# Attention and gated MLP on one core: heads in pairs, 64-row score tiles, and one written order for TensorE

## The chip, the cores and the metric

The kernel runs on one core of a Trainium2 chip. The metric is the device time of one execution in microseconds (us), median of several runs.

## What is computed

Sliding-window attention with ALiBi (a bias that falls linearly with the distance of query and key, with a slope for each head), and behind it a two-layer MLP with a swish gate. Batch 8, 8 heads, 576 tokens, 64 columns a head; 4608 tokens of 512 columns enter the MLP, whose inner width is 2048. All inputs and the output are fp32.

```python
scores = scale * np.matmul(q, k.transpose(0, 1, 3, 2))
slopes = 2.0 ** (-8.0 * (np.arange(H, dtype=np.float32) + 1) / H)
bias = slopes[:, None, None] * (-np.abs(rel).astype(np.float32))[None, :, :]
mask = (rel >= 0) & (rel < window)          # window = 128
scores = np.where(mask, scores + bias[None], -1000000000.0)
attn = np.exp(scores - max); attn = attn / sum(attn)
x = np.matmul(attn, v)                      # to (4608, 512)
h = x @ w_in
g = h * (1.0 / (1.0 + np.exp(-beta * h)))
out = g @ w_out
```

## The kernel before, in words

The work goes batch by batch. `emit_loads` (L72 to L95) brings q, k and v of a batch into bf16 tiles `qs`, `ks`, `vs`, with a cast during the transfer, all issued by GpSimd (POOL); so are both weight matrices (L144, L145). Batch b+1 is loaded while batch b is worked on. The loads, then the weights, stand in POOL's queue ahead of the small identity `identf` (L148) by which TensorE transposes beta (L152).

ALiBi is put into the score product: four more columns (L238, L239, from the tables `QA` and `KBH`) follow the 64 of each head, so that q and k have 68 rows after their transposition. TensorE transposes one head of 128 tokens at a time (L245, L253) into PSUM, and VectorE (DVE) copies eight heads at once to `qT` and `kT` (L248, L256).

For a block `kb` of 128 keys (the fifth has 64) and a pair of heads, two matmuls (L270) give the scores against the key block's own queries and those of the next block, at most 256 columns, in the PSUM tile `sps`, of which there are two. ScalarE (ACT) makes one exponential of both heads (L281, L294), DVE multiplies by a 0/1 mask (L287, L300), and the result `pt` holds probabilities by key. For each block of queries, matmuls with `pt` as the stationary operand (L318, L327) give 64 columns of output and, from a column of ones in `vs`, the sum; DVE divides (L335, L336); four transposes (L345) and a DVE copy (L350) put the 512 columns of these tokens into the ring `XT`.

When 512 tokens are complete, `emit_moe_group` (L176) runs the MLP for them. Stage one: for each of 16 blocks of inner columns, four matmuls of 512 columns to `hps` (L184; two PSUM buffers), a tanh on ACT with a scale per partition (L192), and on DVE (tanh + 1) * h to `gT` (L198). Stage two: for each of four blocks of 128 tokens, 16 matmuls to `ops` (L211; one PSUM buffer), scaling by 0.5 on DVE (L219), and a store on SyncE's queue (SP, L221).

The order on each engine comes from the framework's scheduler, which mixes the instructions of these stages as it lists them. A transpose, score product or pv product of a short block has 64 rows or columns in its operands; all other TensorE work has up to 128 of both and uses the whole array.

Of the kernel before, what the change touches and what calls it, by code (L numbers as in the profile page):

```python
# [14 lines left out]
P = 128  # L15
# [3 lines left out]
def kernel(  # L19
# [16 lines left out]

    NQB = 5
    SPAD = NQB * P
    AUG = 4
    DA = D + AUG  # L40
    DPITCH = 80
# [3 lines left out]
    NTG = (T + TOKG - 1) // TOKG  # L45
    XTR = min(NTG, 3) * TOKG
    slopes = [2.0 ** (-8.0 * (h + 1) / H) for h in range(H)]
    qscale = 1.0 / sqrt(D)

# [4 lines left out]
    beta_sb = const.tile([P, NFF], F32, name="beta_sb")  # L54
    mask = const.tile([P, 2, 2, P], BF16, name="mask")
    QA = const.tile([P, NQB, AUG], BF16, name="QA")
    KB = const.tile([P, NQB, AUG], BF16, name="KB")
    KBH = const.tile([P, NQB, H, AUG], BF16, name="KBH")
    const.seal()

    xt_pool = ctx.enter_context(tc.tile_pool(name="xtbuf", bufs=1))
    XT = xt_pool.tile([P, NDM, XTR], BF16, name="XT")
    xt_pool.seal()
    wt_pool = ctx.enter_context(tc.tile_pool(name="wts", bufs=1))
    W1 = wt_pool.tile([P, NDM, DFF], BF16, name="W1")
    W2 = wt_pool.tile([P, NFF, DM], BF16, name="W2")
    wt_pool.seal()

    make_identity(nc, ident[:])

    stage = ctx.enter_context(tc.tile_pool(name="stage", bufs=2))
    qt_pool = ctx.enter_context(tc.tile_pool(name="qtkt", bufs=2))  # L72

    stage_tiles = {}

    def emit_loads(b):
        qs = stage.tile([P, NQB, H, DPITCH], BF16, name="qs", tag="qs")
        ks = stage.tile([P, NQB, H, DPITCH], BF16, name="ks", tag="ks")
        vs = stage.tile([P, NQB, H, DPITCH], BF16, name="vs", tag="vs")
        for sb in range(NQB):  # L80
            rows = P if sb < 4 else 64
            for src, dst in ((q, qs), (k, ks)):
                nc.gpsimd.dma_start(  # L83
                    out=dst[0:rows, sb, :, 0:D],
                    in_=src[b, :, 128 * sb : 128 * sb + rows, :].rearrange("h p d -> p h d"),
                )
        for h in range(H):
            nc.gpsimd.dma_start(  # L88
                out=vs[:, 0:4, h, 0:D],
                in_=v[b, h, 0:512, :].rearrange("(kb p) d -> p kb d", p=P),  # L90
            )
        nc.gpsimd.dma_start(
            out=vs[0:64, 4, :, 0:D],
            in_=v[b, :, 512:576, :].rearrange("h p d -> p h d"),
        )  # L95
        stage_tiles[b] = (qs, ks, vs)

    nc.vector.memset(mask[:], 1.0)
    nc.gpsimd.affine_select(
        out=mask[:, :, 0, :],  # L100
        in_=mask[:, :, 0, :],
        compare_op=ALU.is_ge,
        fill=0.0,
        base=0,
        pattern=[[0, 2], [1, P]],
        channel_multiplier=-1,
    )
    nc.gpsimd.affine_select(
        out=mask[:, :, 1, :],
        in_=mask[:, :, 1, :],  # L110
        compare_op=ALU.is_ge,
        fill=0.0,
        base=-1,
        pattern=[[0, 2], [-1, P]],
        channel_multiplier=1,
    )

    nc.vector.memset(QA[:, :, 0:2], 1.0)
    nc.vector.memset(KB[:, :, 2:4], 8.0)
    for sb in range(NQB):  # L120
        lo_off = 128 * (sb % 2)
        hi = 256 * (sb // 2)
        nc.gpsimd.iota(
            QA[:, sb, 2:3],
            pattern=[[0, 1]],
            base=-lo_off,
            channel_multiplier=-1,
            allow_small_or_imprecise_dtypes=True,
# [100 lines left out]
    for b in range(B):  # L229
        qs, ks, vs = stage_tiles[b]  # L230
        if b + 1 < B:
            emit_loads(b + 1)
# [155 lines left out]
```

## Time and profile before

| what | value |
|---|---|
| runs of the kernel, us | 450.35, 449.67, 446.89; median 449.67 |
| span of the profiled execution, us | 447.5 (no other time of it is on record) |
| PE, DVE, ACT, POOL busy | 92%, 61%, 39%, 28% of the span |
| mean granted clock of TensorE | 0.934 of full speed |
| bytes read from and written to HBM | 36.71 MB, 9.44 MB |

PE is TensorE's matmul row, PEld its weight loads. A clock of 1.0 is 2.4 GHz and 0.5 is 1.2 GHz; values between are means over a stretch. Matmuls overlap in the pipeline, so the time that one costs is the step from its start to the next start, not its own duration.

### The profile page before, as it was taken

The numbers are of one execution on the slowest core, as the hardware profiler recorded it, in microseconds if no ns is written. First come the engines' busy times: TensorE is split into PE (matmuls) and PEld (weight loads), VectorE is DVE, ScalarE is ACT, GpSimd is POOL, SyncE is SP. The second block draws the span as 40 slices with busy tenths as digits, with TensorE's granted clock in tenths as the row PEclk, the third lists the DMA queues.
The fourth block names the chain that finished last, engine by engine and source line by source line (L and its number), as shares of the span: only waits on it lengthen the run. The fifth ranks groups of instructions, "written<-read, shape, count | busy, mean of one in ns | idle before, by whom it ended". The sixth has DMA issues, their size and how long they took to land.

```text
span 447.5 us, 7410 instructions
## 1 busy us (share of the span) xinstructions
PE 412.8 (92%) x2849; PEld 225.2 (50%) x2849; DVE 275.1 (61%) x764; ACT 174.6 (39%) x305; POOL 124.7 (28%) x174
## 2 busy tenths in 40 slices
PE   3489999899989999999999999999999999999975
PEld 2365455545555465545554556445644465444332
DVE  4465675756765676657496738755777378743531
ACT  0082541535253523543175307540456027522510
POOL 9931998050610507050420507023000000000000
PEclk9855999779998999899999996899999998999999
DMA  9999999362990809062690819018100110001001
GB/s 75 122 200 189 122 148 162 41 41 13 96 106 1 53 26 159 20 41 37 83 94 1 75 51 129 2 10 92 49 0 1 47 48 2 1 25 70 1 23 70
DMA packets 120867, 28.27 MB, mean 63 GB/s; under 512 B 113648, under 2 KB 115712, under 8 KB 120832
## 3 DMA queue, kind: packets, MB, share of 16 engines
q0 software_dynamic: 115616, 18.36, 55.2%
q1 hardware_dynamic: 5216, 9.45, 5.6%
q8 instruction: 22, 0.36, 0.3%
q14 instruction: 13, 0.11, 0.1%
HBM read 36.71 MB, written 9.44 MB: 103 GB/s over the span
## 4 chain that ended last, share of the span: by engine, by line
PE 81%; ACT 7%; DVE 5%; POOL 4%; issue 1%; ACTq 0%
PE hps L184 30%; PE ops L211 28%; PE sps L270 8%; PE pv L327 4%; ACT pt L281 4%; PE pv L318 3%; PE tq L245 3%; PE tk L253 3%; PE xt L345 2%; DVE gT L198 2%; ACT sig L192 2%; DVE osb L219 1%; POOL vs L88 1%; POOL qs L83 1%; ACT pt L294 1%
## 5 line engine op out<-in xcount | busy, mean ns | idle before, releaser
L184 PE MATMUL hps<-XT,W 128*128 128x512 bf16 x576 | 154.8, 398 | 2.2 <-DVE gT L198 1.6
L211 PE MATMUL ops<-W,gT 128*128 128x512 bf16 x576 | 149.9, 379 | 4.8 <-DVE osb L219 3.6
L192 ACT ACTIVATE sig<-hps,beta_h 128x512 bf16<-128x512 f32 x144 | 98.9, 687 | 119.1 <-PE hps L184 111.9
L198 DVE SCALAR_TENSOR_TENSOR gT<-sig,hps 128x512 bf16<-128x512 bf16 x144 | 98.4, 684 | 62.2 <-ACT sig L192 61.3
L281 ACT ACTIVATE pt<-sps 128x512 bf16<-128x512 f32 x96 | 53.8, 596 | 104.4 <-PE sps L270 94.4
L211 PEld LDWEIGHTS <-gT 128*128 128x128 bf16 x576 | 55.6, 97 | 71.8 <-issue 4.8
L184 PEld LDWEIGHTS <-W 128*128 128x128 bf16 x576 | 54.8, 101 | 62.7 <-issue 18.3
L88 POOL DMA_DIRECT2D vs<-in_v_dram x64 | 47.9, 804 | 101.6 <-PE pv L327 100.7
L270 PE MATMUL sps<-qT,kT 68*128 68x256 bf16 (+2 forms) x320 | 62.3, 277 | 8.8 <-ACT pt L281 3.7
L219 DVE TENSOR_SCALAR osb<-ops 128x512 f32<-128x512 f32 x36 | 24.8, 689 | 66.6 <-PE ops L211 61.2
L83 POOL DMA_DIRECT2D qs<-in_q_dram x40 | 35.1, 907 | 69.0 <-PE tk L253 32.5
L327 PE MATMUL pv<-vs,pt 128*128 128x65 bf16 (+1 forms) x320 | 46.0, 212 | 0.3
L318 PE MATMUL pv<-vs,pt 128*128 128x65 bf16 (+1 forms) x256 | 42.9, 214 | 0.0
L287 DVE TENSOR_TENSOR pt<-pt,mask 128x512 bf16<-128x512 bf16 x96 | 38.2, 415 | 3.8 <-ACT pt L281 2.8
L327 PEld LDWEIGHTS <-pt 128*128 128x128 bf16 (+1 forms) x320 | 30.0, 107 | 17.8 <-DVE pt L287 6.2
L270 PEld LDWEIGHTS <-kT 68*128 68x128 bf16 (+1 forms) x320 | 28.6, 107 | 18.7 <-issue 13.8
L83 POOL DMA_DIRECT2D ks<-in_k_dram x40 | 35.1, 917 | 10.0 <-DMA W<-in_moe_w_out_dram 9.8
L245 PE MATMUL tq<-ident,qs 128*68 128x128 bf16 (+1 forms) x320 | 29.2, 224 | 7.6 <-DMA qs<-in_q_dram 7.1
L336 DVE TENSOR_TENSOR xn<-pv,zs 128x256 bf16<-128x256 f32 (+1 forms) x80 | 32.5, 415 | 0.4
L318 PEld LDWEIGHTS <-pt 128*128 128x128 bf16 (+1 forms) x256 | 25.9, 111 | 8.3 <-issue 3.4
L245 PEld LDWEIGHTS <-qs 128*68 128x68 bf16 (+1 forms) x320 | 22.7, 118 | 14.6 <-issue 8.3
L248 DVE COPY qT<-tq 68x1024 bf16<-68x1024 bf16 (+1 forms) x40 | 25.1, 626 | 6.0 <-PE tq L245 5.8
(40 smaller groups left out, 204.9 us busy)
## 6 DMA issues: line engine op xcount, KB each, us to landing
out_dram<-osb SPq DMA_DIRECT2D x36, 256.0 KB, 2.0
vs<-in_v_dram POOLq DMA_DIRECT2D x72, 64.0 KB, 3.0
qs<-in_q_dram POOLq DMA_DIRECT2D x32, 128.0 KB, 4.4
ks<-in_k_dram POOLq DMA_DIRECT2D x32, 128.0 KB, 4.8
W<-in_moe_w_in_dram POOLq DMA_DIRECT2D x1, 2048.0 KB, 14.0
W<-in_moe_w_out_dram POOLq DMA_DIRECT2D x1, 2048.0 KB, 23.9
qs<-in_q_dram POOLq DMA_DIRECT2D x8, 64.0 KB, 4.5
ks<-in_k_dram POOLq DMA_DIRECT2D x8, 64.0 KB, 4.4
```

The costliest lines, as they stand in the source:

```text
L83: nc.gpsimd.dma_start(out=dst[0:rows, sb, :, 0:D], in_=src[b, :, 128 * sb : 128 * sb + rows, :].rearrange("h p d -> p h d"),)
L88: nc.gpsimd.dma_start(out=vs[:, 0:4, h, 0:D], in_=v[b, h, 0:512, :].rearrange("(kb p) d -> p kb d", p=P),)
L184: nc.tensor.matmul(hps[:, 0:gsz], lhsT=W1[:, c, bass.ts(j, P)], rhs=XT[:, c, ringc : ringc + gsz], start=(c == 0), stop=(c == NDM - 1),)
L192: nc.scalar.activation(out=sig[:, 0:gsz], in_=hps[:, 0:gsz], func=ACTF.Tanh, scale=beta_h[:, j : j + 1],)
L198: nc.vector.scalar_tensor_tensor(out=gT[:, j, 0:gsz], in0=sig[:, 0:gsz], scalar=1.0, in1=hps[:, 0:gsz], op0=ALU.add, op1=ALU.mult,)
L211: nc.tensor.matmul(ops_[0:rows, :], lhsT=gT[:, j, i * P : i * P + rows], rhs=W2[:, j, :], start=(j == 0), stop=(j == NFF - 1),)
L245: nc.tensor.transpose(out=tq[0:DA, h, 0:rows], in_=qs[0:rows, sb, h, 0:DA], identity=ident[0:rows, 0:rows])
L270: nc.tensor.matmul(sps[0:nkeys, e, 0:ncols], lhsT=kT[0:DA, h, 128 * kb : 128 * kb + nkeys], rhs=qT[0:DA, h, 128 * kb : 128 * kb + ncols], ...
L281: nc.scalar.activation(out=pt[:].rearrange("p h r q -> p (h r q)"), in_=sps[:].rearrange("p h c -> p (h c)"), func=ACTF.Exp, scale=qscale,)
L287: nc.vector.tensor_tensor(out=pt[:].rearrange("p h r q -> p (h r q)"), in0=pt[:].rearrange("p h r q -> p (h r q)"), in1=mask[:].rearrange( ...
L318: nc.tensor.matmul(pv[0:nq, hl, 0 : D + 1], lhsT=pts[qb - 1][hp][0:P, e, 1, 0:nq], rhs=vs[:, qb - 1, h, 0 : D + 1], start=True, stop=False,)
L327: nc.tensor.matmul(pv[0:nq, hl, 0 : D + 1], lhsT=pts[qb][hp][0:Kc, e, 0, 0:nq], rhs=vs[0:Kc, qb, h, 0 : D + 1], start=first, stop=True,)
```

## The change

The kernel is rewritten. Two heads are transposed together (`T`): a tile of 128 tokens by 128 columns, so head 2p lies in partitions 0 to 63 of the transposed tile and head 2p+1 in 64 to 127. The score product (`SC`) takes two key blocks of one pair of heads: four matmuls with 64 rows each, alternately from the lower and the upper half of the array, into one PSUM tile `sps` of two banks (one bank a head), of which there is one. The fifth key block of all eight heads is a tile of its own (`SC4`). ALiBi is split: the part that depends on the query cancels in the division, the part of the key is a per-partition bias of the exponential, so ACT makes four exponentials for a tile, one for each head and distance. Loads bring fp32 by SP's queue into a ring of 14 buffers, and POOL casts them to bf16; the weights stay on POOL's queue in four pieces each, released by a cast. Output scaling moves from DVE to ACT, `ops` has two PSUM buffers, and there are three output buffers.

PE's order is written out (`manual_schedule`); the other engines keep the scheduler's. Attention steps form the list `att`, in which the score steps of a half batch are merged with the pv products and output transposes of the half batch before. Stage one (`HS`) of a group of 512 tokens alternates with stage two (`OS`) of the group before, four matmuls at a time, and the steps of `att` are spread evenly between them.

```diff
-    def emit_loads(b):
...
-        for sb in range(NQB):
-            rows = P if sb < 4 else 64
-            for src, dst in ((q, qs), (k, ks)):
-                nc.gpsimd.dma_start(
...
+    fst_pool = ctx.enter_context(tc.tile_pool(name="fst", bufs=14))
+    bst_pool = ctx.enter_context(tc.tile_pool(name="bst", bufs=4))
...
+    sig_pool = ctx.enter_context(tc.tile_pool(name="sig", bufs=3))
+    osb_pool = ctx.enter_context(tc.tile_pool(name="osb", bufs=3))
     psum_h = ctx.enter_context(tc.tile_pool(name="psum_h", bufs=2, space=bass.MemoryType.PSUM))
...
+    psum_o = ctx.enter_context(tc.tile_pool(name="psum_o", bufs=2, space=bass.MemoryType.PSUM))
+    psum_s = ctx.enter_context(tc.tile_pool(name="psum_s", bufs=1, space=bass.MemoryType.PSUM))
+    psum_t = ctx.enter_context(tc.tile_pool(name="psum_t", bufs=2, space=bass.MemoryType.PSUM))
...
+    def load_rows(src, b, sb):
+        rows = ROWS[sb]
+        f = fst_pool.tile([P, H, D], F32, name="fst", tag="fst")
+        nc.sync.dma_start(
+            out=f[0:rows],
+            in_=src[b, :, P * sb : P * sb + rows, :].rearrange("h p d -> p h d"),
+        )
+        return f
...
+    def load_qk(b, sb):
+        rows = ROWS[sb]
+        fq = load_rows(q, b, sb)
+        fk = load_rows(k, b, sb)
+        t = bst_pool.tile([P, 2, H, D], BF16, name="bst", tag="bst")
+        nc.gpsimd.tensor_copy(out=t[0:rows, 0], in_=fq[0:rows])
+        c = nc.gpsimd.tensor_copy(out=t[0:rows, 1], in_=fk[0:rows])
...
+    def T(b, sb):
...
+        tps = psum_t.tile([P, 2, NP, P], BF16, name="tps", tag="t")
+        for i in range(2):
+            for p in range(NP):
+                nc.tensor.transpose(
+                    out=tps[:, i, p, 0:rows],
+                    in_=src[0:rows, i, 2 * p : 2 * p + 2, :].rearrange("r h d -> r (h d)"),
+                    identity=ident[0:rows, 0:rows],
+                )
+        nc.vector.tensor_copy(
+            out=qk_tiles[b][:, :, :, P * sb : P * sb + rows], in_=tps[:, :, :, 0:rows]
+        )
...
+    def SC(b, m, p):
+        qk = qk_tiles[b]
+        sps = psum_s.tile([P, 2, 512], F32, name="sps", tag="sps")
+        w = P if m == 0 else 64
+        for kk in range(2):
+            kb = 2 * m + kk
+            for e in range(2):
+                lhsT = qk[64 * e : 64 * e + 64, 1, p, P * kb : P * kb + P]
...
+                nc.tensor.matmul(
+                    o, lhsT=lhsT,
+                    rhs=qk[64 * e : 64 * e + 64, 0, p, P * kb : P * kb + nq],
+                    start=True, stop=True, skip_group_check=True,
+                )
...
+        for e in range(2):
+            h = 2 * p + e
+            nc.scalar.activation(
+                out=pt[:, e, 0:256], in_=sps[:, e, 0:256], func=ACTF.Exp,
+                scale=qscale, bias=bias[:, 0, h : h + 1],
+            )
+            nc.scalar.activation(
+                out=pt[:, e, 256:wid], in_=sps[:, e, 256:wid], func=ACTF.Exp,
+                scale=qscale, bias=bias[:, 1, h : h + 1],
+            )
+        mk = (mask0 if m == 0 else mask1)[:, :, 0:wid]
+        nc.vector.tensor_tensor(out=pt[:, :, 0:wid], in0=pt[:, :, 0:wid], in1=mk, op=ALU.mult)
...
+    def OS(g, i, n):
...
+        for j in range(4 * n, 4 * n + 4):
+            nc.tensor.matmul(
+                ops_[:], lhsT=gT[:, j, i * P : i * P + P], rhs=W2[:, j, :],
+                start=(j == 0), stop=(j == NFF - 1),
+            )
+        if n == 3:
+            osb = osb_pool.tile([P, DM], F32, name="osb", tag="osb")
+            nc.scalar.mul(osb[:], ops_[:], 0.5)
+            row0 = g * TOKG + i * P
+            nc.sync.dma_start(out=out[row0 : row0 + P, :], in_=osb[:])
...
+    for b in range(B):
+        for m in range(2):
+            a = [(None, lambda b=b, sb=sb: T(b, sb)) for sb in ((0, 1, 2), (3, 4))[m]]
+            a += [(None, lambda b=b, m=m, p=p: SC(b, m, p)) for p in range(NP)]
+            if m:
+                a.append((None, lambda b=b: SC4(b)))
+            att.append((None, lambda b=b, m=m: loads_ahead(b, m)))
+            att += merged(a, before)
+            before = pvx(b, ((0, 1), (2, 3, 4))[m])
...
+    with tc.manual_schedule(engines={mybir.EngineType.PE}):
+        load_v(0, 0)
+        load_v(0, 1)
+        c = load_qk(0, 3)
+        load_qk(0, 4)
+        with tc.issue_after(c.ins):
+            for n in range(4):
+                load_w1(n)
+        for sb in (2, 3, 4):
+            c = load_v(0, sb)
+        with tc.issue_after(c.ins):
+            for n in range(4):
+                load_w2(n)
+        done = 0
+        while done < need[0]:
+            att[done][1]()
+            done += 1
+        for g in range(NTG):
+            items = []
+            for j in range(NFF):
+                items.append(lambda g=g, j=j: HS(g, j))
+                if g:
+                    items.append(lambda g=g, j=j: OS(g - 1, j // 4, j % 4))
+            target = need[g + 1] if g + 1 < NTG else len(att)
+            start = done
+            for n, it in enumerate(items):
+                it()
+                while done < start + (target - start) * (n + 1) // len(items):
+                    att[done][1]()
+                    done += 1
         for j in range(NFF):
...
+            OS(NTG - 1, j // 4, j % 4)
```

`PV` and `X` are the pv products with their division and the output transposes of before, `HS` is stage one as before, `need[g]` is the place in `att` at which the tokens of group g are complete, and `pvx` lists the `PV` and `X` steps of some query blocks.

TensorE in the middle of the program, before: a score product (`sps`, which waits for ACT to free one of two buffers) stands among pv products, and 16 matmuls of stage two (`ops`) follow it in a row.

```order
L327 LDWEIGHTS pt_1570 [waits DMASW6_49,DVE_49]
L327 MATMUL pv_1588<-vs_803,pt_1570 128x65 [waits PE_49]
L327 LDWEIGHTS pt_1570
L327 MATMUL pv_1588<-vs_803,pt_1570 128x65 [waits DMASW7_49]
L270 LDWEIGHTS kT_1439
L270 MATMUL sps_1602<-qT_1438,kT_1439 128x256 [waits Activation_49]
L211 LDWEIGHTS gT_1152
L211 MATMUL ops_1321<-W2_74,gT_1152 128x512 [waits DVE_49]
```

The same place in the changed kernel: one score tile, between four matmuls of stage one (`hps`) and four of stage two. Each of the two score rows stands twice, once for each half of the array.

```order
L297 LDWEIGHTS W1_72
L297 MATMUL hps_1672<-XT_71,W1_72 128x512
L196 LDWEIGHTS qkT_1453 [waits PE_49]
L196 MATMUL sps_1680<-qkT_1453 128x2x128 [waits Activation_49]
L196 LDWEIGHTS qkT_1453
L196 MATMUL sps_1680<-qkT_1453 128x2x128
...
L196 MATMUL sps_1680<-qkT_1453 128x256
...
L313 LDWEIGHTS gT_1105
L313 MATMUL ops_1619<-W2_73,gT_1105 128x512
```

A score tile now has MoE work on both sides, and it waits for ACT to free the only buffer.

TensorE in the last group of 512 tokens, before: the last blocks of stage one and the beginning of stage two of the same group, with waits for DVE (`hps` for a free buffer, the weight load of `gT` for its data).

```order
L211 LDWEIGHTS gT_5085
L211 MATMUL ops_5214<-W2_74,gT_5085 128x512
L184 LDWEIGHTS W1_73
L184 MATMUL hps_5206<-XT_69,W1_73 128x512 [waits DVE_49]
...
L184 MATMUL hps_5206<-XT_69,W1_73 128x512
...
L211 LDWEIGHTS gT_5085 [waits DVE_49]
```

The same place in the changed kernel: the last block of stage one of the last group (`hps`), with stage two of the group before (`gT_4234`) around it.

```order
L313 LDWEIGHTS gT_4234
L313 MATMUL ops_4720<-W2_73,gT_4234 128x512
...
L297 LDWEIGHTS W1_72
L297 MATMUL hps_4749<-XT_71,W1_72 128x512 [waits DVE_49]
...
L297 MATMUL hps_4749<-XT_71,W1_72 128x512
```

Stage one of the last group no longer runs alone; stage two of that group follows as one block of 64 matmuls.

GpSimd's queue at the start, before: the end of batch 0's loads, the weights, and the identity for beta's transpose (`identf`) between the first loads of batch 1.

```order
L88 DMA vs_120<-in_v_dram 128x4x64 [waits DMASW1_49]
L92 DMA vs_120<-in_v_dram 64x8x64 [waits DMASW2_49]
L144 DMA W1_73<-in_moe_w_in_dram 128x4x2048 [waits DMASW3_49]
L145 DMA W2_74<-in_moe_w_out_dram 128x16x512 [waits DMASW4_49]
masks.py:197 MEMSET identf_59 16x16
L83 DMA qs_186<-in_q_dram 128x8x64 [waits DMASW5_49]
masks.py:199 AFFINE_SELECT identf_59<-identf_59 16x16 [waits Pool_49]
L83 DMA ks_187<-in_k_dram 128x8x64 [waits DMASW6_49]
```

The same stretch in the changed kernel: casts of q, k and v, each waiting for a load, masks, the identity, and the first quarter of W1 behind the tenth cast.

```order
L123 AFFINE_SELECT mask1_64<-ones_62 128x2x256
L100 CAST bst_136<-fst_132 128x512 [waits DMAHW5_49]
L126 AFFINE_SELECT mask1_64<-ones_62 128x2x64
L129 AFFINE_SELECT mask1_64<-ones_62 128x2x128
masks.py:197 MEMSET identf_59 16x16
masks.py:199 AFFINE_SELECT identf_59<-identf_59 16x16 [waits Pool_49]
L101 CAST bst_136<-fst_134 128x512 [waits DMAHW6_49]
L108 CAST vs0_69<-fst_183 128x8x64 [waits DMAHW7_49]
L108 CAST vs0_69<-fst_186 128x8x64 [waits DMAHW0_49]
L100 CAST bst_193<-fst_189 128x512 [waits DMAHW1_49]
L101 CAST bst_193<-fst_191 128x512 [waits DMAHW2_49]
L148 DMA W1_72<-in_moe_w_in_dram 128x4x512
```

The identity moved ahead of the weights and behind five casts; the weights moved behind ten casts; the loads themselves left this queue.

## Rows read from the trace of the kernel before

**Rows 1.** The page: span, and busy time and share of each engine.

```profile
span 447.5 us, 7410 instructions
...
PE 412.8 (92%) x2849; PEld 225.2 (50%) x2849; DVE 275.1 (61%) x764; ACT 174.6 (39%) x305; POOL 124.7 (28%) x174
```

**Rows 2.** Windows: stretch, length, busy us (instructions) by engine, PE clock, DMA, GB/s.

```profile
0.00:40.00 40.00, 24.75 (x210) 18.61 (x211) 22.53 (x115) 11.17 (x21) 25.62 (x48) 0.74 1.27 144
40.00:410.00 370.00, 359.50 (x2518) 194.89 (x2518) 238.80 (x629) 153.16 (x269) 99.05 (x126) 0.95 0.59 57
410.00:447.50 37.50, 28.56 (x124) 11.73 (x122) 13.76 (x20) 10.30 (x15) 0.00 (x0) 0.98 0.09 35
```

**Rows 3.** Timeline of PE, 120 to 163 us: start, length, line, shapes, count.

```profile
120.41 3.62 PE L211 MATMUL ops<-W,gT 128*128 128x512 bf16 x16
123.86 0.23 PE L327 MATMUL pv<-vs,pt 128*128 128x65 bf16 x2
...
134.42 0.19 PE L318 MATMUL pv<-vs,pt 128*128 128x65 bf16 x1
...
134.63 0.19 PE L327 MATMUL pv<-vs,pt 128*128 128x65 bf16 x1
...
139.48 0.22 PE L318 MATMUL pv<-vs,pt 128*64 128x65 bf16 x1
139.63 0.21 PE L327 MATMUL pv<-vs,pt 64*64 64x65 bf16 x1
...
140.94 1.04 PE L184 MATMUL hps<-XT,W 128*128 128x512 bf16 x4
...
159.84 0.61 PE L253 MATMUL tk<-ident,ks 128*68 128x128 bf16 x8
160.29 0.61 PE L245 MATMUL tq<-ident,qs 128*68 128x128 bf16 x8
...
161.61 0.60 PE L270 MATMUL sps<-qT,kT 68*128 68x256 bf16 x4
162.05 0.61 PE L245 MATMUL tq<-ident,qs 128*68 128x128 bf16 x8
```

**Rows 4.** Timeline of the start; in brackets idle time before, and what ended it.

```profile
21.20 0.28 PE L152 MATMUL bps<-identf,bflat 16*128 16x16 f32 x1 [5.93 <-POOL identf masks.py:199]
...
21.74 1.01 PE L270 MATMUL sps<-qT,kT 68*128 68x256 bf16 x4 [0.27 <-DVE beta_sb L153]
...
23.07 1.08 ACT L281 ACTIVATE pt<-sps 128x512 bf16<-128x512 f32 x2
...
39.95 3.53 PE L184 MATMUL hps<-XT,W 128*128 128x512 bf16 x8
```

**Rows 5.** The page: a DMA queue's packets, and one weight's issue (us to landing).

```profile
q0 software_dynamic: 115616, 18.36, 55.2%
...
W<-in_moe_w_out_dram POOLq DMA_DIRECT2D x1, 2048.0 KB, 23.9
```

**Rows 6.** Groups by form: line, engine, shapes, count, busy us, mean ns, idle before.

```profile
L192 ACT ACTIVATE sig<-hps,beta_h 128x512 bf16<-128x512 f32 x144 | 98.9, 687 | 119.1 <-PE hps L184 111.9 <-DVE gT L198 6.0 <-PE pv L318 1.0
...
L281 ACT ACTIVATE pt<-sps 128x512 bf16<-128x512 f32 x96 | 53.8, 596 | 104.4 <-PE sps L270 94.4 <-PE pv L327 7.3 <-PE pv L318 1.0
...
L83 POOL DMA_DIRECT2D qs<-in_q_dram x40 | 35.1, 907 | 69.0 <-PE tk L253 32.5 <-PE tq L245 29.5 <-DMA W<-in_moe_w_in_dram 7.0
...
L294 ACT ACTIVATE pt<-sps 128x384 bf16<-128x384 f32 x32 | 15.0, 488 | 2.5 <-PE pv L318 1.8
...
L99 POOL TENSOR_SCALAR_AFFINE_SELECT mask<-mask 128x256 bf16<-128x256 bf16 x1 | 0.4, 407 | 0.1
```

**Rows 7.** The chain that ended last, in the last stretch: start, us, what.

```profile
410.89 0.69 ACT sig L192
...
411.61 0.70 DVE gT L198
...
443.62 0.69 DVE osb L219
```

More of the change, by code (lines that the diff above doesn't have):

```diff
@@ L98 @@
[L98 to L116, printed above, removed]
@@ new lines @@
+    for h in range(H):
+        for half in range(2):
+            nc.vector.tensor_scalar(
+                out=bias[:, half, h : h + 1], in0=kpos[:], scalar1=-(REF + half * P),
+                scalar2=slopes[h], op0=ALU.add, op1=ALU.mult,
+            )
+    nc.scalar.activation(out=w4[:], in_=bias[0:64, 0, :], func=ACTF.Exp)
+    for h in range(H):
+        nc.vector.tensor_scalar_mul(A4[:, h % 2, h // 2, :], mask0[0:64, 0, 0:64], w4[:, h : h + 1])
+    for i in range(2):
+        nc.vector.memset(VS[i][:, :, :, D : D + 1], 1.0)
@@ new lines, in X @@
+    def X(b, qb):
+        nq = ROWS[qb]
+        xnv = xns.pop((b, qb))[:].rearrange("p h d -> p (h d)")
+        xt = psum_t.tile([P, NDM, P], BF16, name="xt", tag="t")
+        for c in range(NDM):
+            nc.tensor.transpose(
+                out=xt[:, c, 0:nq], in_=xnv[0:nq, c * P : (c + 1) * P], identity=ident[0:nq, 0:nq]
+            )
+        tok0 = (b * S + P * qb) % XTR
+        n1 = min(nq, XTR - tok0)
+        nc.vector.tensor_copy(out=XT[:, :, tok0 : tok0 + n1], in_=xt[:, :, 0:n1])
+        if n1 < nq:
+            nc.vector.tensor_copy(out=XT[:, :, 0 : nq - n1], in_=xt[:, :, n1:nq])
@@ new lines, with HS @@
+    gts, opss = {}, {}
+    def HS(g, j):
+        if j == 0:
+            gts[g] = gt_pool.tile([P, NFF, TOKG], BF16, name="gT", tag="gT")
+        c0 = (g * TOKG) % XTR
+        hps = psum_h.tile([P, TOKG], F32, name="hps", tag="hps")
+        for c in range(NDM):
+            nc.tensor.matmul(
+                hps[:], lhsT=W1[:, c, bass.ts(j, P)], rhs=XT[:, c, c0 : c0 + TOKG],
+                start=(c == 0), stop=(c == NDM - 1),
+            )
+        sig = sig_pool.tile([P, TOKG], BF16, name="sig", tag="sig")
+        nc.scalar.activation(out=sig[:], in_=hps[:], func=ACTF.Tanh, scale=beta_h[:, j : j + 1])
+        nc.vector.scalar_tensor_tensor(
+            out=gts[g][:, j, :], in0=sig[:], scalar=1.0, in1=hps[:], op0=ALU.add, op1=ALU.mult
+        )
@@ new lines @@
+    att, before = [], []
+    for b in range(B):
[7 more added lines that the diff above has]
+            before = pvx(b, ((0, 1), (2, 3, 4))[m])
+            if b == 0 and m == 1:
+                att += before[:6]
+                before = before[6:]
```

433 lines of the change are left out of this document (171 added, 262 removed).

## The prediction, made before the changed kernel ran

> **What bounds the kernel now.** I read the page first. TensorE (PE) is busy 92% of 447.5 us, VectorE (DVE) 61%, ScalarE (ACT) 39% and GpSimd (POOL) 28% [rows 1]: only PE can be the bound, but a busy PE may still be slow or waiting. So I next took the windows of three stretches [rows 2]: a start of 40 us with PE's clock at 0.74 of full speed, a middle of 370 us at 0.95, and a last 37.5 us in which PE is busy 28.6 us. Then PE's timeline, for the pitch (start to start) of each kind at full clock [rows 3]. A 512-column MoE matmul: 16 from 120.41 to 123.86 us, 0.216. A 128-column transpose: 8 from 159.84 to 160.29, 0.056. A 256-column score matmul: 4 from 161.61 to 162.05, 0.110. A probability-times-V matmul (pv): 7 steps from 134.42 to 134.63, 0.030. When neighbours change the shape of their operands between 128 and 64 rows or columns, the pitch is not 0.030: ten steps that alternate between 128*64 and 64*64 run from 139.48 to 140.94, 0.146 each. Such a change costs 0.116.
>
> With these prices and the counts of the code PE's work is: MoE 1152 x 0.216 = 248.8 us; 512 whole and 128 half transposes of q and k (a half one priced as a pv step) 32.5; scores 192 x 0.110, 64 of 192 columns at 0.082 in proportion, and 64 of 64 columns as pv steps, 28.3; 576 pv 17.3; 160 transposes of the attention output 8.1; and 243 changes of shape in the program's order x 0.116 = 28.2. Sum 363. So 84 us of the span are not PE work at full clock. About 14 us of the work (batch 0's share) lie before the first MoE matmul at 39.95 us [rows 4], so the start holds 26 of the 84; 4 us lie behind the last matmul, from 443.62 on [rows 7]. Of the other 54, the middle's clock takes 0.05 x 370 = 18.5 and the last stretch's 0.8; 35 are waits at full clock. The chain of the last stretch shows one kind: tanh 0.69, then gT 0.70, one behind the other, with PE waiting for both, because no other work is left to mix in [rows 7].
>
> **The change, part by part.** *Head pairs.* A 128x128 transpose now holds two heads of 64 columns: 256 whole and 64 half ones instead of 512 and 128. PE saves 16.3 us of the 32.5, DVE half of its 80 copies.
>
> *Score tiles.* 128 pairs of matmuls read 64 rows of the array, one head in rows 0 to 63 and one in 64 to 127; 64 small ones serve the last key block. The columns are those of before: 28.3 us if each costs what a 256-column one does now. All have a 64-row shape, so there are 307 changes, 64 more: +7.4 us. No row of before has two matmuls in different halves of the array. Bounds: 0.110 for each from above; from below 0.030 for the second of a pair, the smallest step in rows 3, which would give back 128 x 0.08 = 10 us. I take 0.110, the row of the same operation. PE's work is then 363 - 16.3 + 7.4 = 354 us, of which 14 stand ahead of the first MoE matmul and 340 behind it.
>
> *ALiBi as bias.* The augmenting columns and their DVE fills go, off the path. ACT pays: 128 exponentials become 256 of 256 or 192 columns with a bias pointer, plus 8. From 596 ns at 512 and 488 at 384 columns one column is 0.84 ns; the tanh with its pointer takes 687, so a pointer is 91 [rows 6]: 0.47 us for 256 columns, 0.42 for 192. Of two back to back that take 0.59 each, both are done in 1.08 [rows 4], a pitch 0.10 below the duration, so four take about 1.6. ACT's sum is 98.9 for tanh + 192 x 0.47 + 64 x 0.42 + 8 x 0.6 + 36 output scalings that come from DVE x 0.6 = 242 us instead of 175, below 60% of any span here. Hidden, except where one score tile waits for the last (rivals).
>
> *Loads.* 120 fp32 loads go to SP's queue and 120 casts to POOL, which loses the 152 DMA issues of q, k and v and keeps eight for the weights. No cast is in the trace: from below its price is the 0.41 us of a 256-column select [rows 6], from above three to four times that, 1.4; I take twice, 0.8, for 512 columns: 96 us on POOL, hidden under 360. One load has 1024 pieces of 256 bytes. POOL issued as many in 0.91 us, and the transfers kept that pace [rows 6]; from above, 55.2% of 16 engines x 447.5 us over 115616 packets is 34 ns a packet [rows 5], 64 packets an engine, 2.2 us a load. I take 1.2, nearer to the first. SP's stores now stand behind loads that wait for a free buffer; three output buffers, and some 9 us from one store to the next, cover more than 20 us. Without that cover PE would wait for the output PSUM: 1 us for each of 36 stores is the bound that I keep.
>
> The Trainium skill's "SBUF — State Buffer" (Who interferes with whom) says that a VectorE instruction with two SBUF inputs blocks against a GpSimd one that reads SBUF. No run here shows it yet: before, POOL moved no tensor while masks were multiplied. By that rule, as an estimate from the page, each of 72 mask products could wait out a cast; they lie on DVE, at about half its time, and the sum would stay.
>
> *Start.* Before, POOL issues all loads and both weights, and only then makes the identity for beta's transpose, for which PE waits 5.93 us; the scores come at 21.74 and batch 0 runs, much of it at half clock, to 39.95 [rows 4]. W2 needs 23.9 us from issue to landing [rows 5]. After, that identity stands behind POOL's fifth cast: first load 4 us, four more at 1.2, the cast and masks 2: PE starts at 11. But a single score buffer makes each tile wait for the exponentials of the last: 8 tiles x (0.9 of matmuls at half clock + 0.2 + 1.6) = 21.6. Three transposes ahead take 3, and pv products, the next batch's three transposes and the output transposes take 9 behind (half clock). The first MoE matmul comes at 45 us. Bounds: 31 if only the 21 loads at 1.2 and the first quarter of W1 count, 74 at 2.2 us a load and behind all of both weights.
>
> *One order on PE.* From there every score tile, transpose and pv product stands between groups of four MoE matmuls, the first stage alternating with the second stage of the group before, and the last 16 stage-one groups have stage-two work between them. So the clock has no stretch of small work in which to fall (I leave 2 us for its rise after the start), and the chain of rows 7 has cover. What is late next: the handover, where a group's first matmul waits for the last output transpose and its DVE copy, and buffers turned over one step later. I give half of before's 35 us of waits, 18; bounds 0 and the whole 54.
>
> **Sum:** 45 + 340 + 2 + 18 + 4 = 409 us of span. The profiled execution of before has no time on record beside its span of 447.5; the median of three runs is 449.67, 2.2 more. I add 2: 411 us.
>
> **Rivals.** *Pairs run at once.* If the halves of the array work side by side, the second matmul of each pair is free: 96 x 0.110 + 32 x 0.082 = 13 us less, 398. For it: the two heads write different PSUM banks. Against: no row shows it, and two changes of shape per tile remain. The Trainium skill's "TensorE: Matmul & The Clock Gate" (Part 3: Packing small matmuls) has it as its rule: matmuls on different row groups start some 4 ns apart. No run here has shown it yet.
>
> *Late start.* POOL's casts cost 1.4 us or the loads 2.2: the first MoE matmul comes at 64 instead of 45, 430 us. For it: W1 waits for the tenth cast, and small loads share engines with 8.4 MB of weights. Against: PE's own chain hides the first 10 us of such a delay.
>
> *One score buffer becomes the bound (slower).* Place: score tiles with one other attention step between them, about 42 outside batch 0. PE's time from one to the next is 2.3 MoE groups of 0.86, the tile's own 0.67 and a step of 0.2: 2.8 us. If an exponential costs the 596 ns of before whatever its width, and a tanh stands ahead, tile to tile is 0.67 + 0.2 + 0.69 + 2.4 = 4.0: 1.2 x 42 = 50 us, 461. It decides from (449.7 - 411) / 42 = 0.9 us a tile on. For it: ACT runs in one order, and both stages wait there. Against: the slope in rows 6.
>
> *The order doesn't mix.* Clock and waits stay at before's 54 us in place of my 20: 411 + 34 = 445. Against it: the falls of the clock and much of the waiting lie where PE has attention work alone, and no such stretch is left.
>
> **How the numbers follow.** Forecast 0.42, pairs at once 0.34, late start 0.13, score buffer 0.06, no mixing 0.05. About 1% is what a measurement of this kernel can tell from no change. Forecast, pairs and late start are faster (0.89); no mixing is at the border (0.02 faster, 0.03 the same); the score buffer is slower (0.06). The range goes from 390, pairs at once with 8 us fewer waits, to 436, a late start with 6 us more.
>
> **What would show it.** Right: first MoE matmul near 45 us; clock 1.0 from there on; matmuls back to back in the last 14 us; 0.110 between score matmuls and 0.12 more at a change of shape. Wrong: ACT ending PE's waits at the score line for more than 10 us in all; POOL or a load ending PE's waits after 60 us; a store so late on SP that output scaling, and with it PE, waits.

## The result and the profile after

The changed kernel takes 401.62 us (median of 4 runs, 400.38 to 402.21); the kernel before took 449.88 (4 runs). The ratio is 0.8933, 95% interval 0.8892 to 0.8974. The profiled execution has a time of its own, 400.38, beside a span of 398.7: the 2 us around the span were right, and the span is 10 us below the 409 of the sum.

The page of the kernel after, to be read against [rows 1]:

```profile
span 398.7 us, 6725 instructions
...
PE 354.0 (89%) x2529; PEld 174.3 (44%) x2529; DVE 231.1 (58%) x485; ACT 214.5 (54%) x446; POOL 83.2 (21%) x143
...
PE   0447478889999999999999999999999999999996
...
DMA  9999999941987698834137342000000001000112
```

PE is still the bound, but look at where it is not busy: its row reads 0 to 8 for the first nine slices (a slice is 10 us) and 9 from there to the last but one. The DMA row is full for the first eight. The windows answer to [rows 2] (columns as there), cut at the first MoE matmul, 2 us behind the second group's first one (88.3), at about the last score tile and 14 us before the end:

```profile
0.00:53.00 53.00, 22.65 (x198) 15.46 (x199) 24.14 (x69) 15.25 (x38) 23.20 (x46) 0.68 1.20 198
53.00:90.00 37.00, 30.97 (x252) 14.98 (x251) 27.88 (x58) 26.39 (x60) 15.84 (x26) 0.91 1.01 176
90.00:322.00 232.00, 228.08 (x1698) 110.11 (x1698) 152.13 (x310) 143.95 (x306) 44.11 (x71) 1.00 0.42 95
322.00:385.00 63.00, 62.38 (x341) 29.48 (x339) 26.94 (x49) 27.00 (x41) 0.00 (x0) 1.00 0.09 35
```

In 53 us of start PE works 22.65. Behind 90 us it idles 4 us of 232 at a clock of 1.00, and in 322 to 385 us 0.6: the stretches of small work and the chain of [rows 7] are gone. PE's waits in 60 to 398.7 us (us in total, times, longest):

```profile
PE hps L297 <- DVE XT L284: 6.1, 8, 1.6
PE sps L196 <- ACT pt L209: 1.4, 3, 0.7
PE hps L297 <- DVE gT L303: 0.5, 2, 0.3
```

With two more of 0.3 and 0.4 these are all, 8.7 us. The same view of the whole span has for the score tiles

```profile
PE sps L196 <- ACT pt L209: 11.2, 10, 1.7
```

so 9.8 us of their wait for the exponentials lie before 60 us. Now PE's timeline (columns of [rows 3]) at a tile with two key blocks of 256 and 192 columns, at one with two of 256, at a handover, and at the end:

```profile
145.70 0.37 PE L196 MATMUL sps<-qkT 64*128 64x256 bf16 x4
146.00 1.04 PE L313 MATMUL ops<-W,gT 128*128 128x512 bf16 x4
...
161.94 0.39 PE L196 MATMUL sps<-qkT 64*128 64x256 bf16 x4
162.27 1.04 PE L313 MATMUL ops<-W,gT 128*128 128x512 bf16 x4
163.14 0.39 PE L279 MATMUL xt<-ident,xn 128*128 128x128 bf16 x4
164.04 1.02 PE L297 MATMUL hps<-XT,W 128*128 128x512 bf16 x4 [0.52 <-DVE XT L284]
...
383.70 11.17 PE L313 MATMUL ops<-W,gT 128*128 128x512 bf16 x51
```

The tile at 161.94 has four 256-column matmuls and gives way to the next work after 0.33 us; at 0.110 each, as in [rows 3], they alone would take 0.44. The start, SP's queue first and then PE:

```profile
10.27 1.14 SPq L87 DMA_DIRECT2D fst<-in_k_dram  x1
...
23.28 6.42 SPq L87 DMA_DIRECT2D fst<-in_k_dram  x1
29.79 6.42 SPq L87 DMA_DIRECT2D fst<-in_q_dram  x1
36.30 6.42 SPq L87 DMA_DIRECT2D fst<-in_k_dram  x1
...
47.73 1.25 SPq L87 DMA_DIRECT2D fst<-in_q_dram  x1
```

```profile
11.67 0.28 PE L155 MATMUL bps<-identf,bflat 16*128 16x16 f32 x1 [11.67 <-POOL identf masks.py:199]
...
47.23 0.60 PE L169 MATMUL tps<-ident,bst 128*128 128x128 bf16 x4 [4.21 <-POOL bst L101]
...
52.95 1.87 PE L297 MATMUL hps<-XT,W 128*128 128x512 bf16 x4 [0.52 <-DVE XT L284]
```

A load takes SP 1.14 us to issue at 10 us, 6.42 while the four pieces of W2 are on their way (issued from 22.0 us on; 18.9 us from issue to landing, by the page), and 1.25 after. Batch 1's q and k come late, PE waits for their casts, and the first MoE matmul starts at 53.0, not 45.

### The profile page after: what moved, and what is told of

It is laid out like the page before. It is cut to its first block, busy times and chain, and to the rows that moved or that the text cites. A ratio compares the mean times of both kernels' runs of the same rounds, so it can differ in the third digit from the quotient of the medians.

```text
span 398.7 us, 6725 instructions
## 1 busy us (share of the span) xinstructions
PE 354.0 (89%) x2529; PEld 174.3 (44%) x2529; DVE 231.1 (58%) x485; ACT 214.5 (54%) x446; POOL 83.2 (21%) x143
## 4 chain that ended last, share of the span: by engine, by line
PE 79%; DMA 9%; DVE 4%; ACT 3%; SPq 2%; issue 1%; POOL 1%; ACTq 0%
PE ops L313 32%; PE hps L297 31%; DMA fst<-in_k_dram 5%; DMA fst<-in_q_dram 4%; PE sps L196 4%; PE pv L263 4%; PE pv L259 3%; PE tps L169 3%; SPq L87 2%; PE xt L279 2%; DVE gT L303 1%; ACT sig L302 1%; DVE XT L284 1%; ACT pt L209 1%; DVE pt L214 1%
## 5 line engine op out<-in xcount | busy, mean ns | idle before, releaser
L205 ACT ACTIVATE pt<-sps,bias 128x256 bf16<-128x256 f32 x128 | 61.0, 477 | 44.1 <-PE sps L196 44.0
L209 ACT ACTIVATE pt<-sps,bias 128x192 bf16<-128x192 f32 (+1 forms) x128 | 58.2, 455 | 0.0
L214 DVE TENSOR_TENSOR pt<-pt,mask 128x1024 bf16<-128x1024 bf16 (+1 forms) x64 | 43.7, 683 | 15.4 <-ACT pt L209 14.2
L100 POOL CAST bst<-fst 128x512 bf16<-128x512 f32 (+1 forms) x40 | 24.6, 616 | 117.6 <-issue 72.0
L108 POOL CAST vs<-fst 128x512 bf16<-128x512 f32 (+1 forms) x40 | 26.4, 673 | 67.7 <-PE pv L259 24.3
L196 PE MATMUL sps<-qkT 64*128 64x256 bf16 (+1 forms) x256 | 27.3, 287 | 12.8 <-ACT pt L209 11.2
L174 DVE COPY qkT<-tps 128x1024 bf16<-128x1024 bf16 (+1 forms) x40 | 25.4, 635 | 16.2 <-PE tps L169 15.5
L259 PE MATMUL pv<-vs,pt 128*128 128x65 bf16 (+1 forms) x256 | 33.2, 205 | 0.7 <-DVE xn L269 0.6
L169 PE MATMUL tps<-ident,bst 128*128 128x128 bf16 (+1 forms) x320 | 26.0, 230 | 6.8 <-POOL bst L101 4.7
L259 PEld LDWEIGHTS <-pt 128*128 128x128 bf16 (+1 forms) x256 | 22.6, 103 | 14.8 <-issue 5.7
L101 POOL CAST bst<-fst 128x512 bf16<-128x512 f32 (+1 forms) x40 | 24.5, 611 | 18.0 <-DMA fst<-in_k_dram 18.0
## 6 DMA issues: line engine op xcount, KB each, us to landing
W<-in_moe_w_out_dram POOLq DMA_DIRECT2D x4, 512.0 KB, 18.9
```

Source lines behind the costliest of these rows:

```text
L108: return nc.gpsimd.tensor_copy(out=VS[b % 2][0:rows, sb, :, 0:D], in_=f[0:rows])
L169: nc.tensor.transpose(out=tps[:, i, p, 0:rows], in_=src[0:rows, i, 2 * p : 2 * p + 2, :].rearrange("r h d -> r (h d)"), identity=ident[0:r ...
L196: nc.tensor.matmul(o, lhsT=lhsT, rhs=qk[64 * e : 64 * e + 64, 0, p, P * kb : P * kb + nq], start=True, stop=True, skip_group_check=True,)
L205: nc.scalar.activation(out=pt[:, e, 0:256], in_=sps[:, e, 0:256], func=ACTF.Exp, scale=qscale, bias=bias[:, 0, h : h + 1],)
L209: nc.scalar.activation(out=pt[:, e, 256:wid], in_=sps[:, e, 256:wid], func=ACTF.Exp, scale=qscale, bias=bias[:, 1, h : h + 1],)
L214: nc.vector.tensor_tensor(out=pt[:, :, 0:wid], in0=pt[:, :, 0:wid], in1=mk, op=ALU.mult)
```

## The experiments

All times are medians of 4 or 5 runs; the ratio is to the kernel before, with its 95% interval; the two starts are read from PE's timeline.

| kernel | us | ratio | first MoE matmul, us | second group's first, us | span, us |
|---|---|---|---|---|---|
| changed kernel | 401.62 | 0.893 (0.889 to 0.897) | 53.0 | 88.3 | 398.7 |
| order of the four score matmuls | 403.30 | 0.899 (0.895 to 0.902) | 54.0 | 89.5 | 401.4 |
| W2 late | 396.47 | 0.883 (0.879 to 0.887) | 46.9 | 83.6 | 395.6 |
| output transposes first | 402.82 | 0.897 (0.894 to 0.900) | 39.7 | 89.4 | 399.7 |
| both | 396.92 | 0.885 (0.882 to 0.888) | 39.4 | 83.4 | 395.4 |
| both, two score tiles in flight | 392.45 | 0.873 (0.870 to 0.876) | 34.7 | 79.2 | 389.6 |
| one half of the array | 414.78 | 0.922 (0.920 to 0.924) | 53.4 | 92.1 | 413.2 |
| attention in blocks | 495.81 | 1.102 (1.098 to 1.105) | 53.5 | 104.9 | 494.8 |
| loads with a cast by POOL | 401.30 | 0.893 (0.890 to 0.895) | 52.2 | 88.9 | 400.9 |
| stages one behind the other | 434.03 | 0.964 (0.962 to 0.966) | 53.4 | 89.6 | 432.1 |
| handover one set early | 396.39 | 0.881 (0.879 to 0.882) | 53.7 | 89.8 | 394.6 |
| all that helped | 383.81 | 0.853 (0.851 to 0.855) | 33.1 | 76.2 | 381.2 |
| transposes twice | 414.13 | 0.923 (0.918 to 0.928) | 53.9 | 90.8 | 412.0 |

### Do two halves of the array work at once?

Order of the four score matmuls:

```diff
-        for kk in range(2):
-            kb = 2 * m + kk
-            for e in range(2):
+        for e in range(2):
+            for kk in range(2):
+                kb = 2 * m + kk
```

> Score matmuls of one head follow each other, so of the four in a tile only the second and third stand in different halves of the array. If neighbours in different halves run at once, a tile costs three steps in place of two: 64 tiles x 0.110 us = 7 us more than the changed kernel, about 409 us. If they run one behind the other (the term of the prediction), a tile costs four steps either way: 402 us, within 1%.

403.3 us, and the intervals overlap: by the letter the serial theory. But the tiles tell otherwise. A tile of 256 and 192 columns (start, length, as above):

```profile
150.69 0.37 PE L196 MATMUL sps<-qkT 64*128 64x256 bf16 x4
...
150.99 0.39 PE L313 MATMUL ops<-W,gT 128*128 128x512 bf16 x1
```

It takes 0.30, as at 145.70 in the changed kernel: two steps (0.110 + 0.082) and 0.1 for the change of shape behind them, and neither the three nor the four steps that the expectation knew. Both theories took it that only neighbours in the program can overlap, so this run decides nothing between them. The next takes the halves away instead:

```diff
-                lhsT = qk[64 * e : 64 * e + 64, 1, p, P * kb : P * kb + P]
+                lhsT = qk[0:64, 1, p, P * kb : P * kb + P]
...
-                    rhs=qk[64 * e : 64 * e + 64, 0, p, P * kb : P * kb + nq],
+                    rhs=qk[0:64, 0, p, P * kb : P * kb + nq],
```

> Both heads of a pair are scored from the lower 64 partitions, so head 2p is computed twice and head 2p+1 is left out; the number, sizes and order of all instructions stay, but no two score matmuls lie in different halves of the array. If two halves run at once (the rival of the prediction), the second of each pair now costs its own step: 96 x 0.110 + 32 x 0.082 = 13 us more than the changed kernel, about 414 us. If it was one behind the other already (the forecast), 402 us, within 1%.

414.78, 13.2 us more, and the same kind of tile:

```profile
150.85 0.55 PE L196 MATMUL sps<-qkT 64*128 64x256 bf16 x4
151.34 1.04 PE L313 MATMUL ops<-W,gT 128*128 128x512 bf16 x4
```

0.49 in place of 0.30: 0.19 more, the 0.110 + 0.082 of one 256- and one 192-column step. The starts inside the tiles say the same: in the changed kernel's tile 145.701, 145.704, 145.820 and 145.824 us, 3 to 4 ns apart within a pair; on one half 150.854, 150.974, 151.083 and 151.165. The halves work at once, and 13 us of the change's gain are that. The Trainium skill's "TensorE: Matmul & The Clock Gate" (Part 3: Packing small matmuls) states it for matmuls on different row groups, and the 3 to 4 ns here agree.

### What holds the start?

W2 late; output transposes first (the first 512 tokens are then complete sooner in the attention list); and both:

```diff
             for sb in range(3):
-                load_qk(b + 1, sb)
+                c = load_qk(b + 1, sb)
+            if b == 0:
+                with tc.issue_after(c.ins):
+                    for n in range(4):
+                        load_w2(n)
...
-        with tc.issue_after(c.ins):
-            for n in range(4):
-                load_w2(n)
```

```diff
+                before = before[:5] + before[7:8] + before[5:7] + before[8:]
                 att += before[:6]
```

> The four loads of W2 are issued behind the casts of batch 1's first q and k instead of before them. If batch 1's loads are late because W2's transfers hold the DMA engines (each load 6.4 us to issue from 23 to 43 us, 1.1 us before), they take 1.1 us again, PE goes from the transposes at 39.9 us without a wait, and the first MoE matmul comes at about 45 us instead of 53: about 394 us. If the engines are full with other work, or W2 only pushes the loads behind it, the first MoE matmul or the stretch behind it is as late as now: 400 to 403 us.

> The last output transposes that the first MoE group needs stand ahead of the transposes of batch 1. The first MoE matmul comes at about 40 us instead of 53; but batch 1's second and third transposes still wait for casts at 47 and 50 us inside the group, with two or three sets of four MoE matmuls (1.87 us each at half clock) done before: 4 to 5 us gained, about 397 us. If an order of PE is worth nothing while the loads are late, 400 to 402 us.

> W2 late and the output transposes first, together. If the late loads and the order each hide the other, the first MoE matmul comes at about 40 us and nothing waits behind it: 13 us less than the changed kernel, about 389 us. If the loads behind W2 (batch 1's v, fourth and fifth q and k) are now the late ones, PE waits for them between 50 and 65 us and the gain stays at 5 to 8 us: 394 to 397 us.

W2 late gave 5 of the 8 us: its transfers held batch 1's loads. They were not alone: with W2 out of the way the first two of these loads still take SP 5.71 and 5.20 us, from 18.8 to 29.8 us, while W1's pieces are on their way, and the loads of q and k from 33.4 to 41.3 us about 1. The Trainium skill's "DMA: Bandwidth & Descriptors" (Queues, rings and completion order) has each DMA engine take a packet from one queue and then from the next; the 6.42 us of a load of 256-byte pieces beside W2 fit that, but no run here shows single turns.

The other two fell short. With the output transposes first the MoE begins at 39.7 us, 13 us earlier, and the time stays; with both it begins at 39.4, and the time is that of W2 late. The kernel with both:

```profile
39.36 1.87 PE L297 MATMUL hps<-XT,W 128*128 128x512 bf16 x4 [0.52 <-DVE XT L284]
...
51.52 0.39 PE L196 MATMUL sps<-qkT 64*128 64x256 bf16 x4 [1.91 <-ACT pt L209]
...
83.36 1.85 PE L297 MATMUL hps<-XT,W 128*128 128x512 bf16 x4 [1.73 <-DVE XT L284]
```

The second group comes at 83.4, waiting for XT, as it does at 83.6 with W2 late alone. It needs nearly all of batch 1's attention, with only 16 sets of MoE work to lie between it, so score tiles wait for their exponentials again; no wait for a cast stands between 50 and 65 us. For the changed kernel and the four so far that keep both halves of the array the table has the span at the second group's start plus 310 to 312 us: that start, and not the first MoE matmul, is what counts among these five. What sets it was tried next, on top of both:

```diff
-        sps = psum_s.tile([P, 2, 512], F32, name="sps", tag="sps")
+        alt = b < 2 and p % 2
+        pool, tag = (psum_o, "ops") if alt else (psum_s, "sps")
+        sps = [pool.tile([P, 512], F32, name="sps", tag=tag) for _ in range(2)]
```

(`sps4` becomes two tiles of one bank too, with an exponential for each, and `psum_s` has two buffers of one bank.)

> On top of W2 late and output transposes first: in batches 0 and 1, before stage two needs its two PSUM banks, every second score tile uses them, so that two tiles are in flight. If the single score buffer sets the pace in the first two batches (tiles 2.1 us apart, PE waiting 1.0 to 1.9 us for ACT at each), the first MoE matmul comes 4 to 5 us earlier, the second group some 8 us earlier: about 389 us. If ACT itself, the half clock or the loads set it, 395 to 398 us.

392.45: 4.5 us less, half of what was expected. The MoE begins 4.7 us earlier and the second group 4.1. In batch 0 tiles now follow at 24.22, 25.26 and 26.50 us, where the changed kernel has 27.50, 29.61 and 31.71. The single buffer did set the pace of batch 0. In batch 1 something else is late, by PE's waits:

```profile
PE tps L169 <- POOL bst L101: 3.0, 1, 3.0
...
PE tps L169 <- POOL bst L100: 1.7, 1, 1.7
```

These are the casts of batch 1's last q and k (at 49.7 and 53.0 us), whose loads now meet W2, issued from 38.9 us on.

### What is the one order worth?

Attention in blocks, and, with the attention spread, the two stages one behind the other:

```diff
             for n, it in enumerate(items):
+                while n == 4 and done < target:
+                    att[done][1]()
+                    done += 1
                 it()
-                while done < start + (target - start) * (n + 1) // len(items):
-                    att[done][1]()
-                    done += 1
```

```diff
             for j in range(NFF):
                 items.append(lambda g=g, j=j: HS(g, j))
-                if g:
+            if g:
+                for j in range(NFF):
                     items.append(lambda g=g, j=j: OS(g - 1, j // 4, j % 4))
```

> The attention steps of a group stand in one block behind its fourth set of MoE matmuls instead of being spread over 16 or 32 sets; the same instructions otherwise. If the spreading is what covers the waits for the single score buffer and keeps the clock up, each of some 52 score tiles behind the start waits 1.0 to 1.7 us for its exponentials as in batch 0, and the clock falls in some blocks: 52 to 90 us more, 455 to 490 us, slower than the kernel before. If the order is worth little because other steps of the block cover the exponentials, 405 to 420 us.

> Attention stays spread, but the 16 sets of stage one of a group stand together, and the 16 sets of the earlier group's stage two behind them, instead of one by one in turn. If the turn of the stages covers the chain tanh (0.69) and gT (0.68) behind each set, waits of 0.2 to 0.3 us at each stage-one set come back where no attention stands between, in the last group above all: 16 x 0.3 = 5 us there and as much again in the middle groups, 407 to 420 us. If the spread of the attention alone covers them, 400 to 404 us.

In blocks: 495.81, slower than the kernel before. The two largest of PE's waits behind 60 us, then two windows, in a block and behind it:

```profile
PE sps L196 <- ACT pt L209: 34.6, 36, 1.9
PE sps L196 <- DVE qkT L174: 7.0, 9, 1.3
```

```profile
264.00:275.00 11.00, 6.18 (x59) 4.30 (x59) 6.85 (x16) 6.47 (x18) 4.41 (x6) 0.50 1.02 188
...
290.00:306.00 16.00, 16.00 (x76) 7.24 (x75) 6.19 (x9) 7.65 (x12) 0.00 (x0) 1.00 0.09 34
```

PE's waits behind 60 us are 61 us in place of 8.7. Over the whole span PE is idle 96 us in place of 45 and busy 398.6 in place of 354.0, for the same instructions, as the clock falls to its lower level (0.50) in a block and returns behind it: 51.5 + 44.6 = 96, the whole difference of the spans. How much of the 44.6 the waits bring by themselves, as in the next run, was not separated from the clock. So the rival with the single score buffer is true of this kernel where nothing lies between the tiles; the written order is what keeps it away.

Stages one behind the other: 434.03, more than expected. One row explains it:

```profile
PE hps L297 <- DVE gT L303: 22.5, 45, 1.0
```

Stage one waits for tanh and gT at 45 places, half a microsecond each, and PE's busy time grows by 11.4 us on top (365.4), 0.25 a wait, which was not in the expectation. The last matmul before a wait counts to its end, 0.16 us past the start that the next would have had (a MoE matmul lasts 0.379 us, its step is 0.216); the rest of the 0.25 stays open. Alternating the stages is worth 32 us.

### The handover, the loads and the transposes

```diff
-                while done < start + (target - start) * (n + 1) // len(items):
+                while done < min(target, start + (target - start) * (n + 1) // (len(items) - 1)):
```

> The attention steps that a group of MoE needs end one set of four MoE matmuls before the group begins instead of at its end. The changed kernel waits 6.6 us in 9 places for the copy of the last output transpose, 0.6 to 0.7 us at each of seven handovers behind the start; if PE's set of 0.86 us covers that copy, 4 to 5 us less: 397 us. If another wait (gT of the set before, an exponential) takes its place, 400 to 402 us.

396.39, 5.2 us less. The wait of 6.1 us in 8 places behind 60 us has become

```profile
PE hps L297 <- DVE XT L284: 0.7, 1, 0.7
```

Loads as before the change, by POOL, straight into `bst` and `VS`, without `fst` and its casts:

```diff
-        nc.sync.dma_start(
-            out=f[0:rows],
+        return nc.gpsimd.dma_start(
+            out=to,
```

> q, k and v are loaded with a cast during the transfer by POOL's queue, as in the kernel before; no fp32 buffers, no casts on POOL. If the new loads matter only where they meet the weights, everything behind the start runs as in the changed kernel, and the time differs by the start alone: 398 to 408 us. If the fp32 loads on SP are worth much by themselves (POOL waiting for a free buffer with later loads and issues queued behind it), PE waits for transposes in the middle: 415 us or more.

401.30, no difference, and the first MoE matmul at 52.2 us, nearly as late as with SP's queue: the way of loading is worth nothing by itself. A side of it shows in the mask products (line, shapes, count, busy us, mean ns), first of the changed kernel, then of this one:

```profile
L214 DVE TENSOR_TENSOR pt<-pt,mask 128x1024 bf16<-128x1024 bf16 x32 | 23.0, 718 | 10.9 <-ACT pt L209 10.4
...
L214 DVE TENSOR_TENSOR pt<-pt,mask 128x896 bf16<-128x896 bf16 x32 | 20.7, 647 | 4.5 <-ACT pt L209 3.8
```

```profile
L208 DVE TENSOR_TENSOR pt<-pt,mask 128x1024 bf16<-128x1024 bf16 x32 | 22.0, 686 | 11.3 <-ACT pt L203 10.9
...
L208 DVE TENSOR_TENSOR pt<-pt,mask 128x896 bf16<-128x896 bf16 x32 | 20.0, 625 | 4.9 <-ACT pt L203 4.0
```

With casts on POOL the products take 32 and 22 ns longer on average, 1.7 us on DVE in all, which is off the path; the longest of the 64 takes 1078 ns in place of 694. That agrees with the rule of the Trainium skill's "SBUF — State Buffer" (Who interferes with whom) that the prediction weighed; its price is small here.

Last, each transpose of q and k issued twice:

```diff
-            for p in range(NP):
+            for p in (0, 0, 1, 1, 2, 2, 3, 3):
```

> Every transpose of q and k is issued twice into the same place, so that the number of them is that of one head at a time, as before the change; nothing else differs. If PE is the bound behind the start and each transpose costs its step (256 x 0.056 + 64 x 0.030 = 16.3 us, of which the two batches ahead of the first MoE matmul may hide up to 4), the time rises by 12 to 16 us, to 414 to 418 us: the term of the prediction. If transposes lie in PE's spare time, it rises by less than 6 us.

414.13, 12.5 us more. The first MoE matmul comes 0.9 us later and the second group 2.5, so about half of the 5.4 us of transposes ahead of it are hidden. From there to the end the span grows by 10.8 us, the whole price of the 168 + 48 transposes behind it (168 x 0.056 + 48 x 0.030 = 10.8). Not run by themselves were the second `ops` buffer, the output scaling on ACT and ALiBi as a bias; what each is worth stays open.

### A version that beats both

Two score tiles in flight, the handover early, and further:

```diff
+                if b == 1:
+                    with tc.issue_after(c.ins):
+                        for n in range(4):
+                            load_w2(n)
...
             if b == 0:
                 with tc.issue_after(c.ins):
-                    for n in range(4):
-                        load_w2(n)
+                    for n in (2, 3):
+                        load_w1(n)
...
+            if done == 5:
+                beta()
```

(W2 stands behind the casts of batch 1's last q and k, half of W1 behind those of its first three, and `beta()` is beta's transpose and its DVE scaling.)

> On top of the kernel with two score tiles in flight: the handover one set early; W2 behind the casts of batch 1's last q and k, the second half of W1 behind those of its first three; beta's transpose behind the first score tiles. Two score tiles gave 392; the waits for casts (4.7 us behind 50 us) and the seven handovers (4.5 us) go, and PE begins some 4 us earlier, of which 1 us reaches the scores: about 383 us. If the loads only come late at another place, as W2 is needed from about 75 us on, or the handover's wait is replaced, 388 to 392 us.

383.81 us, 0.853 of the kernel before; the page:

```profile
PE 353.6 (93%) x2529; PEld 174.0 (46%) x2529; DVE 229.2 (60%) x485; ACT 214.3 (56%) x454; POOL 85.0 (22%) x143
```

PE's work is the same 354 us; its idle time is 28 us in place of 45.

## Why the prediction came out 10 us high

- **Start, 45 us: wrong, it was 53.0.** The step that failed is the load at 1.2 us. It is right alone (1.14) and wrong beside the weights (6.42 beside W2), outside the bound of 2.2, which came from the whole span's mean. The late-start rival named the sharing of engines, but its load, too, was 2.2. The other terms held: PE starts at 11.67 (11 forecast), batch 0's tiles come 2.1 us apart (2.7), a cast takes 0.61 us (0.8). And the term was the wrong one to ask for: the second group's start decides, and it hides most of a late first matmul, as the output transposes first show.
- **PE's work behind it, 340 us: 13 too much.** Score matmuls were taken as serial; the rival, pairs at once, is shown by the run on one half of the array. The rival's price was right to 0.2 us; its time, 398 against 401.6 measured, also rests on the start and the waits, whose errors nearly cancel. The head pairs' prices (16.3 us in all) are borne out by the doubled transposes. The price of a change of shape held where pv shapes alternate, with steps of 0.147 us as before; a score tile among MoE matmuls pays a little less, 0.096 ahead of it (0.312 in place of 0.216) and 0.093 behind.
- **Clock and waits, 2 + 18: too much.** 8.7 us are waits behind 60 us. Of 53 to 60 us some 4 are lost: PE does 3 us of work there at full pace (two sets of MoE matmuls, three score tiles, four small transposes), at about half pace (1.87 us for four MoE matmuls) and with a wait of 1.7. Half of before's waits was a guess; the order took nearly all but the handover, which the prediction named as what is late next. The rival of an order that doesn't mix is refuted: broken up in two ways, the order costs 32 and 94 us.
- **The sum.** 53.0 + 327 + 8.7 + 4 + 4.2 (the last matmul starts at 394.5) = 397, against a span of 398.7. 8 us too little at the start, 13 too much for the scores and 7 too much for waits and clock nearly make the 10 us. That the forecast came this near is in part luck: with W2 late, where the start is almost the forecast one (46.9 us), the kernel takes 396.5, 14.5 us less than the 411.
- **The test as written.** ACT ends PE's waits at the score line for 11.2 us, above the 10 that should have spoken against the forecast. The threshold had no place in it: 9.8 of these lie in the start, where the sum has them. Nothing of POOL or a load ends a wait of PE behind 60 us, and no store is late. Of the signs of being right, the clock of 1.00 (behind 60 us) and the last 14 us back to back came true; the first MoE matmul at 45 us and 0.110 between all score matmuls did not.
- **ACT's 242 us.** The page says 214.5, yet the groups agree with the terms:

```profile
L205 ACT ACTIVATE pt<-sps,bias 128x256 bf16<-128x256 f32 x128 | 61.0, 477 | 44.1 <-PE sps L196 44.0
...
L209 ACT ACTIVATE pt<-sps,bias 128x192 bf16<-128x192 f32 x64 | 27.5, 430 | 0.0
...
L319 ACT ACTIVATE osb<-ops 128x512 f32<-128x512 f32 x36 | 21.8, 604 | 17.4 <-PE ops L313 16.8
```

  0.477, 0.430 and 0.604 us stand beside 0.47, 0.42 and 0.6. Back-to-back exponentials overlap by some 0.1 us, and the page counts the overlap once.

## What to carry to other kernels

A start is priced by the first moment at which the bound engine has work without a gap, here the second group, and a load's price is its price beside whatever else the DMA engines then carry: put big weights behind the small loads that are needed first. An engine at 89% hides its losses in orders, so try the order by breaking it: alternating the two stages was worth 32 us, more than the transposes saved (12.5) and the halves of the array (13.2) together. And where a step waits for one copy at a seam, an earlier place for the copy removes the wait without a faster copy (5.2 us here).

## What the runs showed of the hardware beyond that

A granted clock of 1.00 in a view is not always a clock that was granted. Between 40 and 60 us it reads 0.50 in the changed kernel and 1.00 in the one with the other order of score matmuls:

```profile
40.00:60.00 20.00, 11.46 (x64) 5.28 (x64) 5.97 (x12) 5.76 (x14) 7.36 (x13) 0.50 1.19 205
```

```profile
40.00:60.00 20.00, 11.57 (x62) 5.62 (x61) 6.00 (x11) 4.93 (x13) 6.66 (x11) 1.00 1.19 205
...
54.03 1.86 PE L297 MATMUL hps<-XT,W 128*128 128x512 bf16 x4 [0.52 <-DVE XT L284]
```

From the first one's start to the last one's end four MoE matmuls take 1.86 us there, as they take 1.87 in the changed kernel, and 1.02 later on (the row at 164.04 above); most steps inside these two sets are 0.427 us in both, and 0.216 later. The trace of that run holds no record of the clock before 61.5 us, and the view reads 1.00 where it has none. In such a stretch the pitch of a known instruction is the better witness.

Two halves of the array also overlap when the program does not alternate between them: with both matmuls of one head listed first, the tile still took 0.30 us. Its starts are 150.688 and 150.695 us for the two 256-column matmuls, then 150.807 and 150.814 for the two of 192, so the second head's first one did not wait for the first head's second.
